# A list of 386 steps put in another order, with the PSUM pool and the copy engine of each step named anew (local attention beside a long convolution, one core)

## The chip, the core and the metric

The kernel runs on one core of a Trainium2 chip. The core has a matrix engine (PE, which multiplies and transposes, and writes to the memory PSUM alone), a vector engine (DVE), a scalar engine (ACT), a general engine (POOL) and a queue engine (SP) that here issues nearly all transfers (DMAs). Each engine works through its own instructions strictly in the order in which the program issues them, and waits for the others through semaphores. The metric is the device time of one execution in microseconds (us); lower is better.

## The reference, cut to what matters

The output has two halves of 576 columns for 2048 positions. The left half, A, is an attention with 32 heads of 18 columns in which each position looks at 8 positions, 2 apart, behind it. The right half, B, multiplies `q` with a causal convolution, as long as the sequence, of a short convolution of `k` times `v`.

```python
def _A_ref(x, wqkv, wo):                       # x: 1 x 2048 x 576
    H = 32; Dh = D // H; W, dil = 8, 2
    q, k, v = split(x @ wqkv)                  # 32 heads of 18
    idx = pos[:, None] - off[None, :]          # off = 0, 2, .. 14
    kg, vg = k[idx], v[idx]
    logits = einsum("bhsd,bhswd->bhsw", q, kg) * scale   # -1e9 where idx < 0
    o = einsum("bhsw,bhswd->bhsd", softmax(logits), vg)
    return o @ wo
def _B_ref(q, k, v, shift_k, ssm_k, ssm_D):    # each 1 x 2048 x 576
    k_shift = sum over 4 taps t of k_pad[:, t:t + S] * shift_k[:, 3 - t]
    kv = k_shift * v
    y = irfft(rfft(kv, 2S) * rfft(ssm_k, 2S))[:S]
    return q * (y + kv * ssm_D)
out = concatenate([A, B], axis=-1)
```

## The kernel before

The program is one straight line of instructions. It is not written out in loops but as a list, `ORDER` (lines 18 to 46), of 386 items; lines 718 to 724 go through it and call one small function per item, and every engine gets its instructions in that order (`manual_schedule`). An item such as `qk.1.0.3:bs` names the function (`qk`), its arguments (1, 0, 3) and after the colon up to two letters. `a` or `b` says from which of the two PSUM pools, `pa` or `pb` (lines 86 and 87, two buffers of two banks each), the step takes its tiles. `s` or `v` says which engine copies the result out of PSUM: `s` is ACT, `v` is DVE. Without a letter the step takes its default; for `evac` (line 101, most steps) that is ACT, for `copy32` (line 364, the transposes) and for `ys` it is DVE. A letter on a step that uses no PSUM, such as `cv.0.0:a`, has no effect.

The steps, by what they compute:

- `lx`, `lwq`, `lwv`, `lk`, `lv`, `lkn`, `lwo` load inputs through SP. `tj`, `tv`, `t0` to `t5`, `tw`, `ia`, `wt`, `sk` make tables; `ia` (line 434) has four PSUM tiles, transposed by PE, and six copies of them on ACT.
- A, first part: `xt.q.k` transposes x (line 369), `qk.comp.cp.j` projects queries (comp 0) or keys (comp 1) for half cp of the heads and quarter j of the positions (line 417), `qt` the remaining heads, `v.c.k` the values, which go to the DRAM buffer `Dv` and come back shifted through `vl` (line 410).
- A, logits: `lm.n.h` (line 513) is one product on DVE, q times shifted keys, into one of three slots `prr` (or, for h = 2, one of two slots `phr`); `lb.n` (line 526) sums it on PE, and frees the slots of `lm.n.0` and `lm.n.1` and after an odd n the `phr` slot. Then `at`, `sm.0.*` and `sm.1.*` (softmax for each half of the positions; `sm.*.4` is the Exp on ACT), `bt`.
- A, output: `pm.c.ct` (line 637) is a product on DVE of a loaded `vl` tile (three slots `vSr`, two `vStr`) with the weights, into one of three slots `Pr`; `ps` sums on PE and copies out; `po.c.t` multiplies by `wo`, copies to one of two slots `sAr`, and after each second one stores to the output.
- B, forward: `cv.c.k` (line 480) is the short convolution, 32 DVE instructions; `sx` and `kp` transform it and `ssm_k` on PE and write to the DRAM buffers `Dx` and `Dk` (`s1_part`, line 450); `kt` transposes `ssm_k` into two slots. `kl.i` and `xl.i` load a group back, each into one of four slots `Wr`; `ks.i.h` and `xs.i.h` (line 589, two PSUM tiles of 576 columns each) are the second transform.
- B, product and back: `gp.i.h` (line 612, two DVE instructions) multiplies the spectra, `gi.i.h` (line 621, two PSUM tiles) transforms back and stores to the DRAM buffer `Dy`; `yl.i` loads from it, again into a `Wr` slot; `ys.i.u` (line 695) is the last transform and the product with `q` on DVE, in one of two slots `ysr`, stored after u = 1. With the letter `s` ACT copies `ys` out first, and DVE multiplies from SBUF.

A slot is handed out when its step is reached in the list; its first writer then waits until the former user is done, for `ysr` and `sAr` until the former store has landed. SP issues transfers in list order and waits at each until its data or its slot is ready, with all later ones behind it.

Of the kernel before, what the change touches and what calls it, by code (L numbers as in the profile page):

```python
# [15 lines left out]


ORDER = """
lx.0 tj lx.1 lx.2 lwq.1 lwv wm.11 tv t0 xt.0.2:av sk:b lk.0 t2 xt.1.2:av lwq.0 xt.1.0:av xt.1.1:bv xt.0.0:s xt.0.1:bv
xt.2.1:s qk.1.1.1:bs xt.2.2:s t3 tw t1 lx.3 cv.0.0:a lv.1 lk.1 qk.1.1.0:bs cv.0.1:b cv.0.2:b cv.0.3:b qk.1.0.0:s  # L20
xt.2.0:as lv.0 v.0.1:b cv.0.4:b v.1.1:bs wt lk.3 v.0.0:a xt.3.0:s cv.0.5:b lk.2 cv.0.6:a cv.0.7:b cv.1.0 qk.0.1.0:b
xt.3.1:b t4 xt.3.2:as cv.1.1 lm.0.1 cv.1.2:b t5 cv.1.3:b qk.0.0.0:a sx.0.0:s qt.1:s cv.1.4:a lm.0.0 v.2.1:as lv.2
sx.1.0:a cv.1.5 cv.1.6 sx.0.1:b qt.0:b sx.0.2:a cv.1.7:a qk.0.1.1 sx.1.1 qk.0.1.3:b v.0.2:s v.1.2:bs lm.0.2 v.1.0:a
sx.1.2:b qk.1.0.1:bs sx.3.0:b cv.2.0:a qk.0.0.1:a v.3.1:a cv.2.1 sx.3.1 sx.2.0:s cv.2.2:a qt.3:as v.2.0:as qk.1.1.3:bs
sx.2.1:s cv.2.3:a lm.1.0 lb.0:a cv.2.4 cv.2.5:b v.2.2:bs cv.2.6 lm.1.1 v.3.2:av sx.2.2:b sx.3.2:b lv.3 cv.2.7:b
qk.0.1.2:a lb.1:b cv.3.0:b lm.2.2 cv.3.1 cv.3.2:b v.3.0:a qk.1.1.2:bs lm.2.1 qk.0.0.3:bs qk.1.0.3:bs lwo sx.4.0:a
cv.3.3:a lm.3.1 qt.2 sx.4.1:b sx.4.2 qk.0.0.2:as cv.3.4:b cv.3.5:b sx.5.0:b lm.2.0 qk.1.0.2 sx.5.1:a lb.2:bs cv.3.6
cv.3.7:a lm.6.0 at.0.0 lkn sx.5.2:av lm.4.2 ia:b lm.3.0 sx.6.0:as sx.6.1:as sx.6.2:s kt.3:b sx.7.0 sx.7.1:a sx.7.2:av
kt.1:bv lb.3:bs kp.1.0:bs kp.1.1:as lm.4.1 lm.4.0 kp.1.2:bs kp.3.0:s kt.0:as kp.3.1:b kp.3.2:s lm.6.2 kt.2:av lb.4:a
kp.0.0 kp.0.1:s lm.6.1 at.0.1 sm.0.0 xl.0 kp.0.2 kp.2.0:av lm.5.1 kp.2.1:s kp.2.2:bs kt.5:as kt.4:s sm.0.1 lb.6:a  # L30
kp.5.0:av kp.5.1:bs lm.5.0 sm.0.2 xl.1 kp.5.2:as kp.4.0:bs kt.6 kp.4.1:a kp.4.2:as sm.0.3 kt.7:s lb.5:s kp.6.0:as
xs.0.0:bv kp.6.1:a xl.2 kp.6.2:as kp.7.0:v kp.7.1:a kp.7.2 lm.7.0 sm.0.4 lm.7.1 xs.1.0:as sm.0.5 xs.0.1 xs.1.1:a
sm.0.6 lb.7:bs sm.0.7 kl.1 sm.0.8 kl.0 kl.3 ks.1.0:s sm.0.9 sm.0.11 sm.0.10 ks.1.1:as ks.0.0 gp.1.0 at.1.0:av vl.0.0
gp.1.1 bt.0.1:v ks.0.1:bs gp.0.0 ks.3.0:bs gi.1.0:as vl.0.1 xs.2.0:b xl.4 xs.2.1:as gp.0.1 xl.3 bt.0.0:bv at.1.1:b
vl.1.2 sm.1.0 ks.3.1:as kl.2 gi.1.1 pm.0.0 gi.0.0:s xs.3.0:a sm.1.1 vl.0.2 ks.2.0:b pm.0.1 xs.3.1:as sm.1.2 gp.3.0
vl.1.0 kl.4 sm.1.3 gi.0.1:bs gp.3.1 pm.0.2 xs.4.0:as gp.2.0 ks.2.1:b ps.0.0:a pm.0.3 sm.1.4 ks.4.0:b xl.7 gp.2.1 kl.7
gi.3.0:a ks.4.1:b gp.4.0 xs.4.1:as vl.1.1 gi.2.0:s pm.1.4 ks.7.0:a xl.5 pm.1.0 ps.0.1:bs ks.7.1:s vl.2.0 gp.4.1 pm.1.1
xs.5.0:as sm.1.5 sm.1.6 xs.7.0:b kl.6 kl.5 gi.2.1:a xs.7.1:bs ps.1.0:v xs.5.1:b ks.5.0:a vl.3.0 xl.6 gi.4.0 ps.1.2:a
gi.3.1:s vl.3.2 pm.1.2 gi.4.1:as ks.5.1:s pm.0.4 sm.1.7 gp.5.0 pm.1.3 sm.1.8 ps.0.2:bs gp.5.1 xs.6.0 yl.3 sm.1.9 yl.2
ps.1.1:a ks.6.0:s po.0.0:s xs.6.1:bs sm.1.10 gi.5.0:a gp.7.0 yl.0 vl.2.1 gi.5.1:bs gp.6.0 po.0.2:a sm.1.11 vl.2.2  # L40
gp.7.1 po.0.1 ys.3.0:v ys.3.1:v yl.1 bt.1.1:as bt.1.0 po.0.3:bs ks.6.1:bs pm.2.0 gi.7.0:as gi.7.1 gp.6.1 pm.2.1
gi.6.0:a po.1.0:bs pm.2.2 ps.2.0:a vl.3.1 gi.6.1:bs pm.2.4 ys.2.0:av ps.2.2:bs pm.2.3 ys.0.0:v ys.2.1:bs ys.0.1:as
po.1.2 ps.2.1:a po.1.1:b po.1.3:bs pm.3.4 pm.3.0 po.2.0 yl.6 yl.4 pm.3.1 po.2.1:s ps.3.0:b pm.3.2 ps.3.2:a po.2.2:b
pm.3.3 ys.6.0:as yl.5 ys.1.0:v ys.1.1:v ps.3.1:as ys.6.1:v po.2.3:v yl.7 po.3.0:a ys.5.0:bv ys.5.1:a po.3.1:b po.3.2:s
ys.4.0:v po.3.3:b ys.4.1:v ys.7.0:a ys.7.1:bs
"""


# [706 lines left out]
```

## Time and profile before

| | |
|---|---|
| median of the runs shown | 233.52 us (232.54 to 233.6, 3 runs) |
| the profiled execution, first to last instruction | 233.3 us |
| ACT busy | 164.7 us |
| PE granted clock, mean | 0.954 of full speed |
| moved by DMA | 60.57 MB, mean 260 GB/s |
| last `pm` ends on DVE | 213.57 us |

The profile page states for each engine the time in which it was busy, and other views tell what ended each wait. An engine that is busy nearly all the time, in the order of the list, sets the time of its stretch; an engine that waits does so for the last of what it needs. Busy time counts overlapping instructions once. The means of single instructions are a little longer than the distance between two of them, since an engine starts the next one before the last result is out.

### The profile page before, as it was taken

The page shows a single profiled execution, that of the slowest core. Times are in us where ns is not written, and L with a number is a line of the kernel's source. Part 1 is how long each engine was busy: PE and PEld are TensorE (multiplying, and loading weights), DVE is VectorE, ACT ScalarE, POOL GpSimd, SP SyncE. Part 2 cuts the span into 40 slices and gives each one's busy share as a digit, 9 for nine tenths or more (in the row PEclk, how much of TensorE's full clock was granted, in tenths as well). Part 3 has the DMA queues.
Part 4 walks back from the last instruction along what each step waited for, and adds up shares of the span by engine and source line. Part 5 has one row for each costly group of instructions (what it writes and reads, how often), then busy time and mean ns, then how long its engine had stood idle before and what let it go on. Part 6 is the DMA issues. An engine that isn't in the chain of part 4 may idle for free. (4 is left out here: it accounts for less than half of the span.)

```text
span 233.3 us, 4423 instructions
## 1 busy us (share of the span) xinstructions
PE 196.2 (84%) x1727; PEld 112.5 (48%) x1736; DVE 200.7 (86%) x199; ACT 164.7 (71%) x241; POOL 22.2 (10%) x53
## 2 busy tenths in 40 slices
PE   7899969999999977959873979668898979896981
PEld 2644524544544444545532456434564656564661
DVE  2679999989596999778969999999999999996533
ACT  2675739677754969487989789899999758535321
POOL 8001540110210110200000000000000010010100
PEclk9999999999999996779998599999999999997999
...
GB/s 221 348 276 393 248 85 106 155 162 48 55 198 268 134 273 327 218 221 211 307 290 207 330 353 326 374 355 400 306 360 299 327 332 379 274 275 339 121 272 214
DMA packets 46965, 60.57 MB, mean 260 GB/s; under 512 B 2368, under 2 KB 40064, under 8 KB 45920
## 3 DMA queue, kind: packets, MB, share of 16 engines
...
q14 instruction: 8, 0.07, 0.1%
...
## 5 line engine op out<-in xcount | busy, mean ns | idle before, releaser
L103 ACT ACTIVATE area<-psB 128x576 bf16<-128x576 f32 (+7 forms) x122 | 85.2, 745 | 32.2 <-PE psB L381 7.6
L103 ACT ACTIVATE area<-psA 128x576 bf16<-128x576 f32 (+7 forms) x105 | 75.6, 760 | 30.7 <-PE psA L381 12.0
L519 DVE TENSOR_TENSOR area<-area 128x4096 bf16<-128x4096 bf16 x16 | 36.4, 2285 | 5.7 <-PE psA L540 3.3
L642 DVE TENSOR_TENSOR area<-area,area 128x4096 bf16<-128x4096 bf16 (+1 forms) x20 | 40.7, 2069 | 0.1
L381 PEld LDWEIGHTS <-area 128*128 128x128 bf16 x160 | 15.5, 98 | 20.0 <-issue 3.0
L594 PEld LDWEIGHTS <-W 128*64 128x64 bf16 x256 | 14.1, 113 | 22.0 <-issue 15.0
L484 DVE TENSOR_TENSOR area<-area,area 128x2304 bf16<-128x2304 bf16 x16 | 21.6, 1362 | 0.8 <-PE psB L456 0.6
L594 PE MATMUL psB<-area,W 128*64 128x288 bf16 x160 | 16.2, 299 | 6.9 <-DMA area<-Dk 3.9
L381 PE MATMUL psB<-area,area 128*128 128x512 bf16 x85 | 20.1, 379 | 0.3
L693 POOL DMA_DIRECT2D area<-in_B_q_dram x8 | 6.0, 747 | 142.8 <-DVE area L706 119.2
L381 PE MATMUL psA<-area,area 128*128 128x512 bf16 x67 | 16.1, 379 | 2.7 <-DVE area L367 2.5
L456 PE MATMUL psB<-area,T 128*128 128x384 bf16 x58 | 14.8, 346 | 2.9 <-ACT area L103 2.7
L456 PEld LDWEIGHTS <-T 128*128 128x128 bf16 x96 | 9.3, 104 | 15.1 <-issue 9.2
L486 DVE TENSOR_TENSOR area<-area,area 128x2304 bf16<-128x2304 bf16 x12 | 16.3, 1356 | 0.3
L629 PEld LDWEIGHTS <-IAt 64*128 64x128 bf16 x256 | 12.4, 94 | 6.9 <-issue 4.0
L680 PEld LDWEIGHTS <-area 128*128 128x128 bf16 x128 | 12.4, 100 | 5.8 <-issue 2.6
L381 PE MATMUL psA<-area,wv 128*128 128x512 bf16 x60 | 13.9, 379 | 0.0
L594 PE MATMUL psA<-area,W 128*64 128x288 bf16 x96 | 10.2, 310 | 4.1 <-ACT area L103 3.6
L381 PEld LDWEIGHTS <-wv 128*128 128x128 bf16 x80 | 7.6, 98 | 9.4 <-issue 0.6
L616 DVE TENSOR_TENSOR area<-area 128x1152 bf16<-128x1152 bf16 x16 | 12.0, 749 | 0.0
L615 DVE TENSOR_TENSOR area<-area 128x1152 bf16<-128x1152 bf16 x16 | 11.9, 746 | 0.0
L456 PE MATMUL psA<-area,T 128*128 128x384 bf16 x38 | 10.0, 364 | 1.8 <-ACT area L103 1.7
...
## 6 DMA issues: line engine op xcount, KB each, us to landing
area<-Dv SPq DMA_DIRECT2D x8, 1054.0 KB, 8.0
...
area<-Dx SPq DMA_DIRECT2D x8, 576.0 KB, 5.7
area<-Dk SPq DMA_DIRECT2D x8, 576.0 KB, 5.3
Dy<-area SPq DMA_DIRECT2D x8, 576.0 KB, 4.6
area<-Dy SPq DMA_DIRECT2D x8, 576.0 KB, 7.0
...
```

Source lines behind the costliest of these rows:

```text
L103: nc.scalar.activation(dst, src, ACT.Copy, **({} if scale is None else {"scale": scale}))
L381: nc.tensor.matmul(ps[:, u, :], w[:, kb, cols[u]:cols[u] + 128], xT[:, kb, t], start=(kb == 0), stop=(kb == 4))
L456: nc.tensor.matmul(ps[:, ri, 0:384], T1[:, ri, :], sf[:, 384 * ch:384 * ch + 384], start=True, stop=not extra)
L484: nc.vector.tensor_tensor(tB if k else tA, kfull[:, 4 * c + 3 - j:4 * c + 7 - j, :], skb[:, j, :].unsqueeze(1).to_broadcast([128, 4, D]), ...
L486: nc.vector.tensor_tensor(tA, tA, tB, ALU.add)
L519: nc.vector.tensor_tensor(prr.get((n, h)), q2[h][:, :, 512 * aq:512 * aq + 512].unsqueeze(1).to_broadcast([128, 4, 2, 512]), kv, ALU.mult)
L594: nc.tensor.matmul(ps[64 * hp:64 * hp + 64, im, 0:HD], W2[:, im, 8 * g + 2 * prl + hp].rearrange("p l f -> p (l f)"), Wt[:, 2 * prl + hp, ...
L615: nc.vector.tensor_tensor(P[:, 0:2], X, K, ALU.mult)
L616: nc.vector.tensor_tensor(P[:, 2:4], X, swap, ALU.mult)
L629: nc.tensor.matmul(ps[:, hp, 0:HD], IAt[r, tab, 4 * g + 2 * hv + u, :], Pp[(i, hv)][r, n, u, :], start=(n == 0), stop=(n == 3), tile_posit ...
L642: nc.vector.tensor_tensor(P, vv, Lt[:, :, 512 * c:512 * c + 512].unsqueeze(2).to_broadcast([128, 2, nd, 512]), ALU.mult)
L680: nc.tensor.matmul(ps[:, di, 0:288], oT[:, 512 * ct + 128 * tt:512 * ct + 128 * tt + 128], wot[:, ct, d0:d1], start=(ct == 0), stop=False)
```

## The change

`ORDER` is replaced by another list of the same 386 steps. Nothing else in the program changes: no function, no tile, no pool and no transfer. Every step of the old list is in the new one; many stand elsewhere, and the letters after the colon differ for most steps that use PSUM. Of the copies out of PSUM these change engine: on DVE are 7 `xt` (6 before), 6 `kt` (4), 3 `ps` (1), 3 `po` (1), 1 `ks` (0), 1 `lb` (0), 1 `wt` (0), 2 `at` (4), and no `kp` (3), `sx` (2) or `v` (1) any more; `xs` (1) and `bt` (3) keep their number; 10 `ys` (4) are copied out by ACT first.

```diff
--- before.py
+++ after.py
@@ -16,33 +16,33 @@
 
 
 ORDER = """
-lx.0 tj lx.1 lx.2 lwq.1 lwv wm.11 tv t0 xt.0.2:av sk:b lk.0 t2 xt.1.2:av lwq.0 xt.1.0:av xt.1.1:bv xt.0.0:s xt.0.1:bv
-xt.2.1:s qk.1.1.1:bs xt.2.2:s t3 tw t1 lx.3 cv.0.0:a lv.1 lk.1 qk.1.1.0:bs cv.0.1:b cv.0.2:b cv.0.3:b qk.1.0.0:s
-xt.2.0:as lv.0 v.0.1:b cv.0.4:b v.1.1:bs wt lk.3 v.0.0:a xt.3.0:s cv.0.5:b lk.2 cv.0.6:a cv.0.7:b cv.1.0 qk.0.1.0:b
-xt.3.1:b t4 xt.3.2:as cv.1.1 lm.0.1 cv.1.2:b t5 cv.1.3:b qk.0.0.0:a sx.0.0:s qt.1:s cv.1.4:a lm.0.0 v.2.1:as lv.2
-sx.1.0:a cv.1.5 cv.1.6 sx.0.1:b qt.0:b sx.0.2:a cv.1.7:a qk.0.1.1 sx.1.1 qk.0.1.3:b v.0.2:s v.1.2:bs lm.0.2 v.1.0:a
-sx.1.2:b qk.1.0.1:bs sx.3.0:b cv.2.0:a qk.0.0.1:a v.3.1:a cv.2.1 sx.3.1 sx.2.0:s cv.2.2:a qt.3:as v.2.0:as qk.1.1.3:bs
-sx.2.1:s cv.2.3:a lm.1.0 lb.0:a cv.2.4 cv.2.5:b v.2.2:bs cv.2.6 lm.1.1 v.3.2:av sx.2.2:b sx.3.2:b lv.3 cv.2.7:b
-qk.0.1.2:a lb.1:b cv.3.0:b lm.2.2 cv.3.1 cv.3.2:b v.3.0:a qk.1.1.2:bs lm.2.1 qk.0.0.3:bs qk.1.0.3:bs lwo sx.4.0:a
-cv.3.3:a lm.3.1 qt.2 sx.4.1:b sx.4.2 qk.0.0.2:as cv.3.4:b cv.3.5:b sx.5.0:b lm.2.0 qk.1.0.2 sx.5.1:a lb.2:bs cv.3.6
-cv.3.7:a lm.6.0 at.0.0 lkn sx.5.2:av lm.4.2 ia:b lm.3.0 sx.6.0:as sx.6.1:as sx.6.2:s kt.3:b sx.7.0 sx.7.1:a sx.7.2:av
-kt.1:bv lb.3:bs kp.1.0:bs kp.1.1:as lm.4.1 lm.4.0 kp.1.2:bs kp.3.0:s kt.0:as kp.3.1:b kp.3.2:s lm.6.2 kt.2:av lb.4:a
-kp.0.0 kp.0.1:s lm.6.1 at.0.1 sm.0.0 xl.0 kp.0.2 kp.2.0:av lm.5.1 kp.2.1:s kp.2.2:bs kt.5:as kt.4:s sm.0.1 lb.6:a
-kp.5.0:av kp.5.1:bs lm.5.0 sm.0.2 xl.1 kp.5.2:as kp.4.0:bs kt.6 kp.4.1:a kp.4.2:as sm.0.3 kt.7:s lb.5:s kp.6.0:as
-xs.0.0:bv kp.6.1:a xl.2 kp.6.2:as kp.7.0:v kp.7.1:a kp.7.2 lm.7.0 sm.0.4 lm.7.1 xs.1.0:as sm.0.5 xs.0.1 xs.1.1:a
-sm.0.6 lb.7:bs sm.0.7 kl.1 sm.0.8 kl.0 kl.3 ks.1.0:s sm.0.9 sm.0.11 sm.0.10 ks.1.1:as ks.0.0 gp.1.0 at.1.0:av vl.0.0
-gp.1.1 bt.0.1:v ks.0.1:bs gp.0.0 ks.3.0:bs gi.1.0:as vl.0.1 xs.2.0:b xl.4 xs.2.1:as gp.0.1 xl.3 bt.0.0:bv at.1.1:b
-vl.1.2 sm.1.0 ks.3.1:as kl.2 gi.1.1 pm.0.0 gi.0.0:s xs.3.0:a sm.1.1 vl.0.2 ks.2.0:b pm.0.1 xs.3.1:as sm.1.2 gp.3.0
-vl.1.0 kl.4 sm.1.3 gi.0.1:bs gp.3.1 pm.0.2 xs.4.0:as gp.2.0 ks.2.1:b ps.0.0:a pm.0.3 sm.1.4 ks.4.0:b xl.7 gp.2.1 kl.7
-gi.3.0:a ks.4.1:b gp.4.0 xs.4.1:as vl.1.1 gi.2.0:s pm.1.4 ks.7.0:a xl.5 pm.1.0 ps.0.1:bs ks.7.1:s vl.2.0 gp.4.1 pm.1.1
-xs.5.0:as sm.1.5 sm.1.6 xs.7.0:b kl.6 kl.5 gi.2.1:a xs.7.1:bs ps.1.0:v xs.5.1:b ks.5.0:a vl.3.0 xl.6 gi.4.0 ps.1.2:a
-gi.3.1:s vl.3.2 pm.1.2 gi.4.1:as ks.5.1:s pm.0.4 sm.1.7 gp.5.0 pm.1.3 sm.1.8 ps.0.2:bs gp.5.1 xs.6.0 yl.3 sm.1.9 yl.2
-ps.1.1:a ks.6.0:s po.0.0:s xs.6.1:bs sm.1.10 gi.5.0:a gp.7.0 yl.0 vl.2.1 gi.5.1:bs gp.6.0 po.0.2:a sm.1.11 vl.2.2
-gp.7.1 po.0.1 ys.3.0:v ys.3.1:v yl.1 bt.1.1:as bt.1.0 po.0.3:bs ks.6.1:bs pm.2.0 gi.7.0:as gi.7.1 gp.6.1 pm.2.1
-gi.6.0:a po.1.0:bs pm.2.2 ps.2.0:a vl.3.1 gi.6.1:bs pm.2.4 ys.2.0:av ps.2.2:bs pm.2.3 ys.0.0:v ys.2.1:bs ys.0.1:as
-po.1.2 ps.2.1:a po.1.1:b po.1.3:bs pm.3.4 pm.3.0 po.2.0 yl.6 yl.4 pm.3.1 po.2.1:s ps.3.0:b pm.3.2 ps.3.2:a po.2.2:b
-pm.3.3 ys.6.0:as yl.5 ys.1.0:v ys.1.1:v ps.3.1:as ys.6.1:v po.2.3:v yl.7 po.3.0:a ys.5.0:bv ys.5.1:a po.3.1:b po.3.2:s
-ys.4.0:v po.3.3:b ys.4.1:v ys.7.0:a ys.7.1:bs
+lx.0 tj lx.3 lx.1 lwq.1 wm.11:a tv t2 t0 xt.0.1:bs xt.0.0:av xt.0.2:b sk:a lwq.0 xt.1.0:bs t5 lk.0 lwv xt.3.0:b
+xt.1.1:as lv.0 xt.3.1:as t3 qk.1.0.0:b t1 xt.3.2:b tw lx.2 cv.0.0 cv.0.1 qk.0.1.0:a lk.1 cv.0.2 wt:v xt.1.2:as cv.0.3
+t4 qk.0.0.0:b qk.1.1.1:b qk.1.1.3:a xt.2.0:bv cv.0.4 lk.2 cv.0.5 xt.2.2:bv cv.0.6 cv.1.0 qt.1:a xt.2.1:a qk.1.1.0:b
+cv.0.7 qt.0:a cv.1.1 qt.3:b cv.1.2 qk.0.0.1:a cv.1.3 sx.0.0:a lm.2.0 lv.2 qk.0.1.1:b v.0.0:b cv.1.4 cv.1.5 cv.1.6
+sx.0.1:b qk.1.0.3:a lm.0.0 lk.3 lm.0.2 lv.1 lm.0.1 sx.1.0:a qk.0.1.3:b sx.1.1:a sx.0.2:b cv.1.7 qk.1.0.1:a sx.1.2:b
+cv.2.0 cv.2.1 cv.2.2 qk.1.0.2:b v.0.1:a qk.1.1.2:a cv.2.3 v.0.2:b cv.2.4 v.1.2:a lb.0:b sx.2.0:a sx.2.1:b sx.2.2:a
+cv.2.5 v.1.0:b lm.1.1 sx.3.0:a qk.0.0.3:a cv.2.6 sx.3.1:b v.1.1:b sx.3.2:a v.2.0:b lm.1.0 cv.2.7 lv.3 cv.3.0 sx.4.0:a
+cv.3.1 lb.1:b lm.3.0 v.2.2:b v.3.2:a cv.3.2 sx.4.1:b sx.5.0:a lm.2.2 lm.2.1 v.2.1:b sx.4.2:a sx.5.1:b v.3.1:a v.3.0:b
+sx.5.2:bs cv.3.3 qt.2:a qk.0.1.2:a cv.3.4 qk.0.0.2:a cv.3.5 cv.3.6 lm.6.2 lb.2:b lwo cv.3.7 sx.6.0:a sx.7.0:a sx.6.1:b
+lkn lm.3.1 lb.3:b lm.4.2 sx.6.2:a lm.4.0 sx.7.1:b at.0.1:bs sx.7.2:bs at.0.0:as kt.6:as kt.3:bs kp.6.0:a xl.0 lm.4.1
+sm.0.0 lm.6.1 kp.6.1:b lb.4:a sm.0.1 kp.6.2:b lm.6.0 kp.3.0:a kp.3.1:a kt.1:b kp.3.2:a kt.7:a lm.7.0 lb.6:b sm.0.2
+kp.7.0:bs xl.6 kp.7.1:a lm.5.0 kp.7.2:b kt.5:bv kp.1.0:a kp.1.1:b kp.1.2:b sm.0.3 sm.0.4 xl.1 kp.5.0:bs kp.5.1:b
+lm.5.1 kt.2:a lb.5:av lm.7.1 sm.0.5 kp.5.2:a kp.2.0:as sm.0.6 kp.2.1:b kt.4:bv sm.0.7 kp.2.2:a kt.0:a lb.7:b xs.1.0:a
+sm.0.8 vl.1.0 kp.0.0:b kp.0.1:b kp.0.2:a at.1.0:a at.1.1:b kp.4.0:b kp.4.1:a kp.4.2:a sm.0.9 xs.0.0:bs vl.0.0 sm.0.10
+xs.1.1:a sm.0.11 sm.1.0 bt.0.0:b bt.0.1:b pm.1.0 pm.1.1 kl.0 xs.0.1:a pm.0.0 ia:b kl.1 ks.0.0:a ks.0.1:b ks.1.0:a
+sm.1.1 ks.1.1:b gp.0.0 ps.1.0:as xl.2 gp.0.1 gp.1.0 vl.0.1 vl.1.2 vl.0.2 xs.6.0:b gi.0.0:a gp.1.1 kl.6 sm.1.2 xl.4
+xs.6.1:b xs.2.0:a kl.2 pm.0.1 sm.1.3 vl.3.0 ks.6.0:b ps.0.0:a vl.1.1 gp.6.0 gi.0.1:b xs.2.1:av kl.3 ks.6.1:av sm.1.4
+ks.2.0:b xl.7 ks.2.1:b gi.1.0:a xl.3 gp.6.1 gi.1.1:b sm.1.5 gi.6.0:a pm.0.2 gp.2.0 gp.2.1 gi.6.1:b ks.3.0:a pm.1.4
+xs.3.0:b ks.3.1:a xs.4.0:b pm.0.3 vl.3.2 xl.5 sm.1.6 xs.4.1:a kl.4 ps.1.2:bv xs.3.1:b kl.7 gi.2.0:a vl.2.0 gp.3.0
+pm.0.4 vl.2.2 gi.2.1:b gi.3.0:a gp.3.1 ks.4.0:b gi.3.1:a ks.4.1:b ps.0.1:a ps.0.2:a ks.7.0:b pm.1.2 ks.7.1:a gp.4.0
+pm.1.3 gp.4.1 kl.5 ps.1.1:bv xs.7.0:a yl.3 sm.1.7 xs.5.0:b xs.7.1:a po.1.2:b ks.5.0:a sm.1.8 gp.7.0 sm.1.9 vl.2.1
+gi.4.0:b yl.0 gi.4.1:a gp.5.0 po.1.0:b sm.1.11 xs.5.1:a yl.2 sm.1.10 ks.5.1:b gp.7.1 bt.1.1:av yl.1 gp.5.1 ys.0.0:as
+bt.1.0:bs pm.2.0 po.1.1:b ys.0.1:a pm.2.1 po.1.3:b gi.7.0:a gi.7.1:b gi.5.0:a gi.5.1:b pm.2.4 vl.3.1 po.0.0:a po.0.1:a
+pm.2.2 ps.2.0:b yl.6 ps.2.2:a pm.2.3 pm.3.4 ys.2.0:as ys.2.1:b po.0.2:b pm.3.0 ps.2.1:a ys.3.0:as po.0.3:b yl.5
+po.2.0:b pm.3.1 ys.3.1:as yl.7 ys.1.0:bs po.2.2:b ps.3.0:b ps.3.2:a pm.3.2 ys.1.1:as po.2.1:b pm.3.3 ys.5.0:bs
+ys.5.1:as yl.4 po.2.3:as ps.3.1:av ys.7.0:as ys.7.1:bv ys.6.0:bv po.3.0:av po.3.1:av ys.6.1:bs po.3.2:bv ys.4.0:b
+po.3.3:a ys.4.1:a
 """
 
 
```

## Prediction, made before the changed kernel was run

> **What bounds the kernel now.** I read the page first, then the busy time by stretches, the waits of DVE, and the order of instructions in time. The new list gives the same work to the same engines, so what can change is waiting alone.
>
> ```profile
> span 233.3 us, 4423 instructions
> PE 196.2 (84%) x1727; PEld 112.5 (48%) x1736; DVE 200.7 (86%) x199; ACT 164.7 (71%) x241; POOL 22.2 (10%) x53
> ```
>
> DVE is the busiest engine, and its share is an average. By stretches (columns: length, busy PE, weight loads, DVE, ACT, POOL, granted clock, DMA share, GB/s):
>
> ```profile
> 26.00:133.10 107.10, 92.02 (x683) 48.05 (x690) 95.25 (x76) 78.29 (x106) 12.95 (x25) 0.92 0.67 201
> 133.10:213.60 80.50, 66.45 (x792) 42.32 (x789) 79.95 (x77) 65.69 (x111) 2.23 (x3) 0.99 0.96 336
> 213.60:233.30 19.70, 13.82 (x112) 9.80 (x110) 7.45 (x11) 5.57 (x8) 0.75 (x1) 0.93 0.72 214
> ```
>
> From 133.1 us to the last `pm` (213.6) DVE never stops: 79.95 of 80.5. Before that it idles 11.85 of 107.1 us, and behind it lies a tail of 19.7 us in which no engine is full. The waits of DVE (us in total, times, longest) and one of them in the order of time say why:
>
> ```profile
> DVE area L706 <- DMA out_dram<-area: 4.1, 1, 4.1
> DVE area L519 <- PE psA L540: 3.3, 2, 2.4
> DVE area L706 <- ACT area L103: 2.8, 1, 2.8
> DVE area L105 <- PE psA L456: 2.8, 2, 1.8
> DVE area L519 <- ACT area L103: 2.0, 2, 1.8
> ```
>
> ```profile
> 71.34 1.02 ACT L103 ACTIVATE area<-psB 128x1024 bf16<-128x1024 f32 x1 [1.09 <-PE psB L381]
> 72.40 2.29 DVE L519 TENSOR_TENSOR area<-area 128x4096 bf16<-128x4096 bf16 x1 [1.76 <-ACT area L103]
> ```
>
> `lm` waits for `lb` (L540) to free a slot. The second wait needs nothing: `lm.2.1` reads the first quarter of the keys, but starts when ACT's copy of `qk.1.1.2`, a later quarter of the same tile, is done (72.36). So an `lm` waits for every `qk.1` of its half listed before it.
>
> **The measure.** I add up, along each list, the row means of what DVE, ACT and PE do. Old list: DVE 211.2, ACT 186.0; new: DVE 210.6, ACT 188.2. A few copies on DVE have no row of their form: `lb` (512 columns) I take at 0.67 between 0.42 (256) and 0.75 (576); `wt` at 0.5 from the same two. DVE's listed work passes faster than its sum, since neighbours overlap: in the last stretch listed 85.6 take 79.95 busy, a factor of 0.934.
>
> **Stage 1, to listed 17.9 (`xt.2.0`): +1.3.** New, `xt.3.0` is copied by DVE before `t3`, and on PE it lies behind `sk`, whose third tile waits for ACT's first copy. `xt.0.1`'s copy (1.02) now lies before that on ACT, so `t3` starts near 11.6, not 11.50; its Sin waits for it; `tw` ends and `cv.0.0` starts at 18.7 (18.42 before), with 0.7 less DVE work done. `xt.2.0` costs another 0.4, as PE gets there at 25.2. Its loads do not decide: `lx.2` has 6.0 MB before and in it, some 20.5 us at the 302 GB/s of the first 24.6 us. DVE is at 25.9 where it was at 24.6. On POOL `lwv`'s memset (1.05) moves behind `t0`, so `ident` is ready earlier; it costs and gains nothing, since the first transposes wait for `lx.0` (5.94) and `ident` was there at 4.05. The loads of `q` on POOL wait for slots of `qtr`, four of them, as before.
>
> **Stage 2, to listed 117.9 (the first `pm`): -4.5.** Before: 108.5 us, 11.0 of them in waits of 0.2 us and more. I walk the new list with PE at 0.9 of its listed price (17.3 listed take 15.4 us from `lb.1` to `qk.1.0.2` before). No `lm` then finds a `qk.1` unfinished: the last two stand 4 and 8 us ahead. Waits I find: `lm.3.0` for `lb.1` 1.1; `lm.6.2` for `qt.2`, listed four steps ahead, 1.2; `lm.3.1` for `lb.2` 0.6; `lm.4.2` for `lb.3`, which needs the `lm.3.1` just before it, 0.7; `kt.7` for ACT's copy of `kp.3.1` 1.1; `at.1.0`, behind `xs.1.0` and `kp.0` on PE, 1.8. Together 6.5 for 11.0. Behind a waiting `lm` stand only `cv` and `sm`, whose readers (`sx`, `at`) have PE work ahead of them. Its bounds: no wait at all (-9.7 with stage 1) and as much as before (+1.3). `ia` (34 transposes on PE, six copies on ACT) leaves this stage. The first `pm` starts at 129.9, not 133.1.
>
> **Stage 3, to the last `pm`: +2.1.** `ia` moves here, after the third `pm`: six ACT copies at 0.91 (5 took 4.69), 5.5 us, covered by three `pm` (2.2 each, 6.7 in all). Uncovered it would delay `gp` by all of 5.5. Then ACT has 38 pairs of 576-column copies, and
>
> ```profile
> 157.19 1.34 ACT L103 ACTIVATE area<-psA 128x576 bf16<-128x576 f32 x2
> 158.25 1.36 ACT L103 ACTIVATE area<-psB 128x576 bf16<-128x576 f32 x2
> 159.31 1.39 ACT L103 ACTIVATE area<-psA 128x576 bf16<-128x576 f32 x2
> ```
>
> shows a pair each 1.06. With an Exp (1.8), three `ps` and small ones that is 47.7, against DVE's 52.8 x 0.934 = 49.3 up to `pm.2.0`: ACT nearly sets the pace, and in places does. `gp.0.0` waits for `ks.0.1` 0.9, `ps.1.2` on DVE 0.6, `gp.3.0` for `xs.3.1` 1.1, `gp.4.0` for `ks.4.1` 1.2. Behind `gp.0.0` stand `gp.0.1`, `gp.1` and `pm.0.1`; PE needs the first for `gi.0.0`, but has `xs.6.0` ahead of it. Listed 84.4 x 0.934 + 3.8 = 82.6, for 80.5. Bounds: ACT's pairs at 1.06 throughout and no wait, 78.8; each pair at the 1.19 of an unqueued one, 5 us more on ACT, 86.
>
> **Loads in stage 3: +1.9.** Between listed 118 and 140 the new list orders 9.6 MB, the old one 7.3; `vl.3.0`, used last of all, is fetched here. Before, 130 to 170 us ran at 357 GB/s (busy share 0.94), at which 9.6 MB take 26.9 us against 25.0 of DVE's way. Bounds: 0 (at 400 GB/s, the fullest slice of the page, 24 us) and 4 (at 330). I take the row with the same mixture. The Trainium skill ("DMA: Bandwidth & Descriptors", section "Where 436 GB/s comes from") names about 358 GB/s per core for the memory's side and 435 for the ports; by the first the term is 1.9, by the second 0, and this trace's slices up to 400 lie between.
>
> **The tail: -4.2.** Before, two stores lie on the chain that ended last:
>
> ```profile
> 205.75 5.31 DMA out_dram<-area
> ...
> 219.02 5.22 DMA out_dram<-area
> ```
>
> The second holds `ys.5.0`, which needs the slot of `ys.6`, stored just before. In the new list ten `ys` after the last `pm` become eight and halves of `ys`, `po` and `ps` go to ACT and DVE in turn. From the last `pm`: `ps.3.1` on PE 1.0, copied by DVE 1.2; `ys.6.0` waits for the store of `ys.5` (issued 1.2 us after the `pm`, 4.3 to landing), to +6.2; behind it on DVE the copies of `po.3.0` and `po.3.1` stand until +7.7; `ys.4.0` waits for the store of `ys.7` to +9.7; `ys.4.1` ends at +11.5; the last store lands 4.0 later. 15.5 for 19.7; with stores of 5.3 us, 18.2.
>
> **Sum.** -3.2 (stages 1 and 2) +2.1 +1.9 -4.2 = -3.4, and +0.9 for hand-offs below 0.2 us (stage 2 idled 11.85 with 11.0 in named waits): 230.8 for 233.3. The profiled execution lies 0.2 under the median, so 231.0.
>
> **Rivals.**
> *Loads late (slower).* SP issues in list order, and a `Wr` slot is only refilled when its reader on PE is done. `xl.6` takes one of four slots some 20 us before the others, and `vl.3.0` one of three `vSr` slots until the end. That leaves `xl.3` 6.8 us and `kl.4` 6.1 us from slot to use; `kl.3` and `kl.5` are alike.
>
> ```profile
> area<-Dv SPq DMA_DIRECT2D x8, 1054.0 KB, 8.0
> ...
> area<-Dx SPq DMA_DIRECT2D x8, 576.0 KB, 5.7
> area<-Dk SPq DMA_DIRECT2D x8, 576.0 KB, 5.3
> ```
>
> The loads of 576 KB from `Dx` and `Dk` take 5.7 and 5.3 us; if the crowd lifts them above 6, each comes late, at 8.0 (the big `Dv` loads) by some 1.8; behind a late `ks` stand PE's later steps, ACT's copies of them and then `gp` and `pm`, so four of them add up to 7 us: 238. For it: the bytes. Against: DMA already ran at 0.96 with DVE at 99%. Chance 0.30.
> *The tail stays.* Stores of 5.3 us keep it at 18.2: 233.7. For it: the two on the chain; against: the median of 3.7. Chance 0.17.
> *No crowd.* Without the load term and the hand-offs: 228.2. Chance 0.13.
> That the change does nothing can't be: the list is the order of issue. The letters on `cv` fall away without effect.
>
> **How the numbers follow.** My forecast has 0.40; its own range is 229 to 233.5. About 0.5% (1.17 us) is what a measurement tells from no change, so faster is below 232.35, slower above 234.7. Faster: 0.32 of the forecast, 0.13 without crowd, 0.04 of the tail, 0.49. Same: 0.08 + 0.06 = 0.14. Slower: 0.30 + 0.07 = 0.37. The range, 227 to 239, leaves out the ends of the first rival and of the third.
>
> **What would show it.** Right: first `pm` on DVE near 130; an `lm` never released by ACT's copy of a `qk.1`; `ia` beside three `pm`; DVE idle about 4 us from there to the last `pm` near 214; a tail near 15.5, its waits on stores. Wrong: waits of PE (L594) on `Dk` or `Dx` above 3 us in stage 3 (first rival), or PE behind DVE by more than the named waits in stage 2, which my walk would not see.

## The result, and the profile after

The changed kernel takes 244.75 us (median of 4 runs, 243.15 to 247.37); the kernel before, beside it on the same chip, 233.03 (4 runs, 232.28 to 233.6). The ratio is 1.05, interval 1.0427 to 1.0573: slower by 11.7 us, where a gain of 2.5 had been forecast. Below, medians leave out two executions above 310 us (the profiled one of the single letter and one of `lb.4` ahead) and hold one of 375.63 us of the kernel before, while ratios and their intervals leave out every execution more than 1.5% above the fastest of its kernel, so that the two can differ by a microsecond. The page of the changed kernel begins:

```profile
span 243.7 us, 4442 instructions
...
PE 200.8 (82%) x1736; PEld 115.2 (47%) x1736; DVE 199.6 (82%) x202; ACT 166.2 (68%) x244; POOL 21.7 (9%) x53
```

DVE and ACT are as busy as before to within 1.5 us; PE is busy 4.6 us longer with the same work. The busy time by stretches, cut at the prediction's marks (copy of `xt.2.0`, first `pm`, end of the last `pm`; columns as in the prediction), of the changed kernel:

```profile
24.50:140.30 115.80, 96.70 (x691) 48.99 (x691) 96.05 (x75) 75.80 (x103) 11.82 (x17) 0.91 0.64 186
140.30:229.20 88.90, 72.73 (x822) 48.23 (x820) 79.01 (x78) 72.83 (x121) 2.24 (x3) 0.92 0.92 322
229.20:243.70 14.50, 9.85 (x88) 7.01 (x86) 8.00 (x13) 3.10 (x5) 0.75 (x1) 1.00 0.75 225
```

| | before | predicted | after |
|---|---|---|---|
| to listed 17.9 (`xt.2.0`) | 24.6 | 25.9 | 24.5 |
| from there to listed 117.9 (the first `pm`) | 108.5 | 104.0 | 115.8 |
| from there to the last `pm`, loads included | 80.5 | 84.5 | 88.9 |
| tail | 19.7 | 15.5 | 14.5 |

The marks are amounts of listed work on DVE. In the kernel before, 133.1 us is where DVE has done as much listed work as stands ahead of the new list's first `pm`; its own first `pm` comes later, at 143.37. The column before is of an execution of 235.0 us (every time on record lies 1.7 us above its span), so the columns add up to 10.4 us between them and not to the 11.7 of the medians.

So most was lost ahead of the first `pm`, where the forecast had its gain. The longest waits of DVE and PE in the changed kernel (us in total, times, longest):

```profile
DVE area L519 <- PE psA L540: 8.2, 1, 8.2
...
PE psA L501 <- DMA area<-in_B_ssm_k_dram: 6.5, 4, 2.7
...
DVE area L519 <- ACT area L103: 5.4, 1, 5.4
...
PE psB L381 <- DVE area L367: 4.4, 2, 4.0
```

In the first, `lm.6.0` waits for `lb.4`; in the third `lm.0.0` waits for a `qk.1`, which no `lm` was to do. Behind each stands a wait of PE, and the experiments below show that these two cost most of what was lost.

*PE's wait for a copy.* In the order of time, DVE and PE of the changed kernel:

```profile
25.38 0.61 PE L375 MATMUL psA<-ident,area 128*128 128x128 bf16 x8
...
25.83 0.81 PE L381 MATMUL psB<-area,area 128*128 128x512 bf16 x3
...
28.64 1.35 DVE L484 TENSOR_TENSOR area<-area,area 128x2304 bf16<-128x2304 bf16 x1
...
29.91 0.68 DVE L367 TENSOR_SCALAR area<-psA 128x512 int32<-128x512 int32 x1
...
30.65 3.15 PE L381 MATMUL psB<-area,area 128*128 128x512 bf16 x7 [4.01 <-DVE area L367]
...
47.59 2.29 DVE L519 TENSOR_TENSOR area<-area 128x4096 bf16<-128x4096 bf16 x1 [5.43 <-ACT area L103]
```

The copy at 29.91 is that of `xt.2.1`. PE had transposed it by 26, but on DVE it stands behind the instructions of several `cv`, and `qk.1.1.0` on PE waits for it from 26.6 to 30.65. It does not need it: `qk.1.1.0` reads the first quarter of the positions, and `xt.2.1` writes the third, which PE reads from 51.96 on (`qk.1.0.2`). The wait is of the kind that the prediction found for `lm.2.1`. `xT` holds five blocks of 2048 columns, and `xt.2.1` writes columns 1024 to 1535 of blocks 2 and 3; of the matmuls of `qk.1.1.0` those on blocks 0, 1 and 2 run, and the fourth, the one on block 3, waits (x3 and x7 above). In the same way the second matmul of `qt.1` waits for `xt.2.0`. That fits a dependency taken over the whole stretch from the first column written to the last, which includes the first quarter of block 3; no run takes the dependency away. The seven matmuls that follow take 3.15 us, 0.45 each; ten of the same form take 2.32 at 37.06. The stretches of that time, of the changed kernel, say why (the granted clock is the third figure from the right):

```profile
26.60:30.60 4.00, 0.04 (x1) 0.00 (x0) 4.00 (x6) 0.36 (x2) 0.00 (x0) 0.85 0.00 0
30.60:36.10 5.50, 5.45 (x13) 1.92 (x13) 5.43 (x5) 1.16 (x2) 0.00 (x0) 0.50 0.37 109
36.10:42.00 5.90, 5.90 (x29) 2.77 (x28) 5.83 (x4) 4.23 (x8) 0.00 (x0) 0.99 0.00 0
```

After the hole of 4 us the clock is 0.50 for 5.5 us, in which PE does work of 2.75: the hole costs 4.0 + 2.75, and 0.87 more for a wait on `xt.2.0`'s copy before it, 7.6 in all. PE is then full to 88 us and makes up nothing.

*The late load.* SP, PE and DVE of the changed kernel:

```profile
91.44 4.50 SPq L264 DMA_DIRECT2D area<-in_B_ssm_k_dram  x5
...
104.29 0.33 PE L501 MATMUL psA<-ident,area 128*128 128x128 bf16 x1 [2.72 <-DMA area<-in_B_ssm_k_dram]
...
110.42 2.29 DVE L519 TENSOR_TENSOR area<-area 128x4096 bf16<-128x4096 bf16 x1 [8.24 <-PE psA L540]
```

`ssm_k` is ordered at 91.44 (82.39 before): its place is free only when PE, now late, has done the last projection, and `lwo` stands ahead of it on SP. `kt.6` (L501) follows at once on PE, where `ia` stood in between before, and waits 6.5 us for it in four pieces; `lb.4` stands behind `kt.6` and `kt.3`, and `lm.6.0` behind `lb.4`. The first load from `Dk`, which needs all of it, is then issued at 141.82 (127.42 before), and the first `gp` starts at 148.3 (134.9).

### The profile page after: what moved, and what is told of

It reads as the page before. It is cut to its first block, busy times and chain, and to the rows that moved or that the text cites. A ratio compares the mean times of both kernels' runs of the same rounds, so it can differ in the third digit from the quotient of the medians.

```text
span 243.7 us, 4442 instructions
## 1 busy us (share of the span) xinstructions
PE 200.8 (82%) x1736; PEld 115.2 (47%) x1736; DVE 199.6 (82%) x202; ACT 166.2 (68%) x244; POOL 21.7 (9%) x53
## 4 chain that ended last, share of the span: by engine, by line
PE 39%; DMA 31%; ACT 12%; DVE 8%; issue 7%; SPq 1%; DVEq 0%; ACTq 0%
ACT area L103 10%; PE psB L381 9%; DMA Dx<-area 7%; DMA area<-Dk 7%; PE psA L381 6%; DMA out_dram<-area 5%; DMA area<-in_B_v_dram 4%; DMA area<-in_A_wqkv_dram 3%; DMA area<-Dx 3%; PE psA L456 3%; PE psB L456 3%; PE psB L594 2%; DMA Dk<-area 2%; PE psA L594 2%; PE psA L629 2%
## 5 line engine op out<-in xcount | busy, mean ns | idle before, releaser
L103 ACT ACTIVATE area<-psA 128x576 bf16<-128x576 f32 (+9 forms) x120 | 83.9, 740 | 32.4 <-PE psA L381 7.9
L103 ACT ACTIVATE area<-psB 128x576 bf16<-128x576 f32 (+5 forms) x111 | 80.4, 765 | 36.6 <-PE psB L381 14.9
L381 PE MATMUL psB<-area,area 128*128 128x512 bf16 x70 | 17.9, 404 | 4.4 <-DVE area L367 4.4
L381 PE MATMUL psA<-area,area 128*128 128x512 bf16 x90 | 20.7, 379 | 0.0
L594 PE MATMUL psA<-area,W 128*64 128x288 bf16 x128 | 13.5, 319 | 3.7 <-DMA area<-Dk 1.2
L456 PE MATMUL psB<-area,T 128*128 128x384 bf16 x46 | 12.2, 351 | 4.3 <-ACT area L103 4.2
L680 PE MATMUL psB<-wv,area 128*128 128x288 bf16 x80 | 13.4, 297 | 1.3 <-ACT area L103 1.3
L615 DVE TENSOR_TENSOR area<-area 128x1152 bf16<-128x1152 bf16 x16 | 12.0, 749 | 3.1 <-ACT area L103 3.0
L381 PE MATMUL psB<-area,wv 128*128 128x512 bf16 x60 | 13.9, 379 | 0.0
L456 PE MATMUL psA<-area,T 128*128 128x384 bf16 x50 | 12.1, 333 | 0.9 <-ACT area L103 0.5
```

What stands on the lines that cost most here:

```text
L103: nc.scalar.activation(dst, src, ACT.Copy, **({} if scale is None else {"scale": scale}))
L381: nc.tensor.matmul(ps[:, u, :], w[:, kb, cols[u]:cols[u] + 128], xT[:, kb, t], start=(kb == 0), stop=(kb == 4))
L456: nc.tensor.matmul(ps[:, ri, 0:384], T1[:, ri, :], sf[:, 384 * ch:384 * ch + 384], start=True, stop=not extra)
L594: nc.tensor.matmul(ps[64 * hp:64 * hp + 64, im, 0:HD], W2[:, im, 8 * g + 2 * prl + hp].rearrange("p l f -> p (l f)"), Wt[:, 2 * prl + hp, ...
L615: nc.vector.tensor_tensor(P[:, 0:2], X, K, ALU.mult)
L680: nc.tensor.matmul(ps[:, di, 0:288], oT[:, 512 * ct + 128 * tt:512 * ct + 128 * tt + 128], wot[:, ct, d0:d1], start=(ct == 0), stop=False)
```

## The experiments

The kernels are timed beside the kernel before; its medians were 233.91 us (first set), 233.00 (second), 233.09 (third) and 232.45 (fourth).

**The copies of xt.2 on ACT.**

```diff
-xt.2.0:bv ... xt.2.2:bv ... xt.2.1:a
+xt.2.0:bs ... xt.2.2:bs ... xt.2.1:as
```

> The new list, with the copies of xt.2.0, xt.2.1 and xt.2.2 on ACT and not on DVE (3 letters). Theory A (in the new kernel PE waits 4.0 and 0.9 us at 24 to 31 us for these copies, which stand on DVE between the cv, and everything that PE does up to the load of ssm_k comes that much later): the two waits go, lm.0.0 waits under 1.5 us and not 5.4, the load of ssm_k is issued near 87 and not 91.4, the time falls by 3 to 5 us, to about 240. Rival B (the end is set by the loads in the stretch of the products, whatever comes before): the waits go too, but the time falls by less than 1 us.

236.69 us (235.94 to 239.57), ratio 1.0112 (1.0053 to 1.0171). Three letters take back 8.1 of 11.7 us by the medians and 9.0 by the ratios, more than I had given them, since I had not yet seen the clock behind the hole. Both waits of PE and that of `lm.0.0` are gone, `ssm_k` is ordered at 85.00; `lm.6.0` still waits 7.3 for `lb.4`.

**One of the three.**

```diff
-xt.2.1:a
+xt.2.1:as
```

> The changed kernel with one letter other: xt.2.1 is copied by ACT, not by DVE behind six cv; xt.2.0 and xt.2.2 stay on DVE. Theory A (this one copy ended 4 us after PE needed it, and PE, full from there to 88 us, never made it up): most of what the three letters brought, -6 to -7 of 8.1; PE's wait of 4.0 gone, the load of ssm_k issued near 86. Rival D (the three copies cost DVE's own time, 0.68 each and the waits beside them): a third of it, -2.7.

236.43 (median of three, 235.79 to 238.29), ratio 1.0197 (1.0137 to 1.0256). By the ratios, 1.05 and 1.0197, that is 7.1 us less (9.0 with three letters), by the medians 8.3 (8.1). One copy of 0.68 us, in its place in DVE's queue, makes most of the first cause. That its wait is gone is not shown by a trace of this kernel; only the time speaks. Rival D, DVE's own time, falls: a third was expected of it.

**DVE's wait alone.**

```diff
-sx.0.1:b qk.1.0.3:a lm.0.0 lk.3 lm.0.2 lv.1 lm.0.1 sx.1.0:a
+sx.0.1:b lm.0.0 lk.3 lm.0.2 lv.1 lm.0.1 qk.1.0.3:a sx.1.0:a
```

> The new list, with qk.1.0.3 moved from ahead of lm.0.0 to behind lm.0.1. Theory A with the needless dependency (lm.0.0 waits for the copy of a later quarter of the keys): lm.0.0 no longer waits 5.4 us; but PE does the same work in the same time, so the load of ssm_k comes where it was and the time falls by under 1.5 us: DVE's wait moves to the next lm that waits for lb. If DVE's own work set the time (theory of the prediction), it would fall by about 5 us.

243.71 (243.1 to 244.49), ratio 1.0414 (1.0357 to 1.0471): -1.0 by the medians, -2.0 by the ratios. The wait of 5.4 us of `lm.0.0` disappears and the time moves little: `cv.1.7` now waits 3.5 for a load of `v`, which SP issues right behind a store that needs PE's values (44.40 us), and `lm.6.0` waits 6.8. DVE's longest waits show where PE is late; they are not what is to be mended.

**The load of wo behind that of ssm_k.**

```diff
-cv.3.6 lm.6.2 lb.2:b lwo cv.3.7
+cv.3.6 lm.6.2 lb.2:b cv.3.7
...
-kt.5:bv kp.1.0:a
+kt.5:bv lwo kp.1.0:a
```

> The new list, with lwo (six transfers on SP) moved from directly ahead of the load of ssm_k to behind kt.5. Theory A: ssm_k is issued some 3 us earlier (88.5, set by the last projection on PE), kt.6 waits 3 to 4 us less for it, lm.6.0 waits about 5 us and not 8.2, the time falls by 2 to 4 us. Rival B: less than 1 us. If SP is not what holds the load (its slots are), the issue moves by less than 1 us and so does the time.

241.35 (240.29 to 243.34), ratio 1.0331 (1.0263 to 1.04): -3.4, as theory A has it. `ssm_k` is ordered at 87.27, PE waits 1.9 for it, `lm.6.0` 2.9, and the first `pm` starts at 135.8.

**The tables of ia as cover.** `ia` moves from behind the first three `pm` to the place where PE waits for `ssm_k`.

```diff
-at.0.0:as kt.6:as
+at.0.0:as ia:b kt.6:as
```

> The new list, with ia moved back to where the old list has it in kind: behind at.0.0, ahead of the first kt, while ssm_k is on its way. Theory A (kt waits 6.5 us for ssm_k because nothing stands between): PE does ia in this wait, lb.4 and lm.6.0 come no later than before (wait 7 to 9 us), and the first gp no longer has ia's 5.6 us of ACT ahead of it; it gains only if ia and not the load of the first Dk group (landed at 146.3) held gp: 0 to 1 us. Rival C (ia in the product stretch costs its ACT time): it falls by 4 to 6 us.

241.81 (241.09 to 243.52), ratio 1.0352 (1.0291 to 1.0413): -2.9, between the two theories. PE's wait for `ssm_k` is filled, but DVE waits 8.9 for `ia`'s last tile (a fifth one, besides the four copied on ACT, which DVE copies itself) and PE 6.1 on the first load from `Dk`.

**Both causes taken out.** The first and the fourth edit together.

> Both edits at once: the three copies of xt.2 on ACT, and the load of wo behind kt.5. Theory A (PE was held by DVE's copies of xt.2, and the load of ssm_k arrives late behind that of wo with nothing for PE between it and kt.6): alone the edits brought 8.1 and 3.4 us, but the first already moves the issue of the ssm_k load from 91.4 to 85.0, so they overlap: 233 to 235 us, the wait of lm.6.0 on L540 down from 7.3 to about 3, first pm near 130. Rival C (what is left after the copies is the amount of PE and ACT work around kp, not the landing of ssm_k): no further gain, 236 to 237, with PE's wait on ssm_k gone but ACT or PE busy throughout.

234.01 (231.29 to 236.04, 10 runs), ratio 1.004 (0.998 to 1.01). Four edits of 386 steps take back 10.7 of 11.7 us, and the result can't be told from the kernel before. The edits alone brought 8.1 and 3.4 by the medians, 9.0 and 3.9 by the ratios, so they overlap by 0.8 to 2.2. Of this kernel, the stretches at the same marks, and two at the time of the former hole:

```profile
24.50:128.80 104.30, 92.50 (x683) 47.99 (x688) 94.87 (x73) 77.61 (x106) 11.40 (x17) 0.93 0.70 208
128.80:215.10 86.30, 71.77 (x836) 48.89 (x834) 78.92 (x79) 73.80 (x122) 2.24 (x3) 0.94 0.95 330
215.10:232.60 17.50, 10.40 (x72) 6.90 (x71) 7.89 (x12) 1.95 (x3) 0.75 (x1) 0.87 0.63 182
```

```profile
26.60:30.60 4.00, 3.95 (x19) 1.76 (x18) 3.96 (x4) 3.92 (x8) 0.00 (x0) 1.00 0.00 0
30.60:36.10 5.50, 5.50 (x27) 2.54 (x26) 5.43 (x5) 3.40 (x5) 0.00 (x0) 1.00 0.39 109
```

PE is full and its clock 1.00. The second stage takes 104.3 us, where the prediction's walk had 104.0; DVE idles 9.4 of it. `qk.0.0.1`, the first `qk` behind the former hole, starts on PE at 29.30 instead of 37.06: 7.8 us, for the 7.6 counted above. `lm.6.0` still waits 3.5, as expected, and `ssm_k` is ordered at 79.46.

**lb.4 ahead of the transposes.** The kernel of the last run, with PE's order changed so that no sum of logits stands behind `kt.6`.

```diff
-at.0.0:as kt.6:as kt.3:bs kp.6.0:a xl.0 lm.4.1 sm.0.0 lm.6.1 kp.6.1:b lb.4:a sm.0.1
+at.0.0:as xl.0 lm.4.1 sm.0.0 lm.6.1 lb.4:a kt.6:as kt.3:bs kp.6.0:a kp.6.1:b sm.0.1
```

> As the run before, and lb.4 stands ahead of kt.6, kt.3, kp.6.0 and kp.6.1 on PE, so that no sum of logits stands behind a transpose that waits for ssm_k. Theory A: the wait of lm.6.0 on L540 is below 1 us and the first pm on DVE comes about 3 us earlier, but the chain over ssm_k, Dk and the first kl is as long as before, so the time moves by -1 to -3 against the run before. Rival C (the chain over ssm_k sets the first gp, DVE's wait is only a symptom): within 0.5 us of the run before, the wait reappears in front of the first gp.

233.3 (median of nine, 231.62 to 236.2), ratio 1.0048 (1.0005 to 1.0091): against the run before -0.7 by the medians and +0.2 by the ratios, no difference. The wait of `lm.6.0` is gone, but the first `pm` starts at 128.6 instead of 128.8, since three copies of `kt` on DVE now wait 1.6, 1.4 and 1.7 ahead of it. That is rival C's time, though it had the wait return in front of the first `gp`: with `ssm_k` early, DVE's wait was a symptom.

**A big load later.** On the kernel with both causes taken out:

```diff
-sm.1.3 vl.3.0 ks.6.0:b
+sm.1.3 ks.6.0:b
...
-vl.2.1 gi.4.0:b
+vl.2.1 vl.3.0 gi.4.0:b
```

> As the first run of this set, and the load vl.3.0 (1054 KB) moves from the third pm to behind vl.2.1, some 35 us later. Rival B (the prediction's rival of late loads: bytes ahead of xl.3, kl.3 and kl.4 make these late): the waits of L594 on Dx and Dk shrink from about 7 us to 4, time -2 to -3 against the first run. Theory A': the loads are late because their Wr slots are freed late, not because of the bytes: -0.5 to +0.5.

233.73 (231.15 to 235.04), ratio 1.0024 (0.9979 to 1.0069): -0.3, no difference. PE's wait on `Dx` shrinks from 2.2 to 1.6 and DVE's wait behind it from 2.3 to 0.7, but then PE waits 6.0 on a load from `Dy`, and DVE 3.8 behind that. Rival B, the bytes of `vl.3.0`, falls.

**Three loads better placed.** The kernel with `lb.4` ahead, with `vl.3.0` later as above, and:

```diff
-ks.2.0:b xl.7 ks.2.1:b gi.1.0:a xl.3
+ks.2.0:b xl.3 ks.2.1:b gi.1.0:a xl.7
...
-ys.1.1:as po.2.1:b pm.3.3 ys.5.0:bs ys.5.1:as yl.4
+ys.1.1:as yl.4 po.2.1:b pm.3.3 ys.5.0:bs ys.5.1:as
```

> The list of e6_lb4_first with three loads moved: vl.3.0 behind vl.2.1, xl.3 and xl.7 change places (xl.3 is used first), yl.4 directly behind ys.1.1. Theory H (what the repaired list still loses from the first gp on are three late loads: PE's 2.1 us wait on Dx, some of the 2.3 on Dy, and the 3.2 us of DVE in the tail): 230.5 to 232, faster than the kernel before by 0.5 to 1%. Rival I (these waits lie beside ACT's pace of copies, or turn into others, as moving vl.3.0 alone did): 233 to 234.

235.41 (232.27 to 238.09, 12 runs), ratio 1.008 (1.0034 to 1.0125): by the ratios 0.7 us above the kernel without these moves (1.0048), and the intervals overlap; by the medians 2.1, timed on another chip. Theory H falls, and rival I's 233 to 234 is missed too, on the slow side. The trace shows no wait of PE on `Dx` above 1 us any more, and one of 5.0 on `Dy` instead; but its execution, at 232.45, is one of the fastest of the twelve, so it does not show where the others lose time. That stays open.

**The new end in the kernel before.** The last 30 steps, from `pm.3.4` on, in the changed order with its letters, but for the loads `yl.6` and `yl.5`, which stand behind `po.2.0`; the beginning of it:

```diff
-pm.3.4 pm.3.0 po.2.0 yl.6 yl.4 pm.3.1 po.2.1:s ps.3.0:b pm.3.2 ps.3.2:a po.2.2:b pm.3.3 ys.6.0:as
+pm.3.4 pm.3.0 po.2.0:b yl.6 yl.5 pm.3.1 yl.7 ys.1.0:bs po.2.2:b ps.3.0:b ps.3.2:a pm.3.2 ys.1.1:as
...
```

> The kernel before with the last 30 steps (from pm.3.4 on) in the changed kernel's order with its letters. The prediction's tail term (ten ys after the last pm become eight, halves go to ACT and DVE in turn): the tail is 15 to 16 us for 19.7 and the time 228.5 to 230.5. Rival (the tail is short in the changed kernel only because its stage 3 was long and the back transforms were done by then): 232 to 234.

236.01 (233.97 to 236.54), ratio 1.0123 (1.0041 to 1.0205): slower by 3.0. Its last `pm` ends at 221.2, and the span at 234.8: the tail is 13.6 for 19.7, shorter than I had claimed. But the `ys` that have left it stand between the last `pm`s, and DVE waits there for ACT's copies of them:

```profile
213.27 0.46 DVE L706 TENSOR_TENSOR area<-area,area 128x576 bf16<-128x576 bf16 x1 [3.08 <-ACT area L103]
213.64 2.28 DVE L642 TENSOR_TENSOR area<-area,area 128x4096 bf16<-128x4096 bf16 x1
218.63 0.46 DVE L706 TENSOR_TENSOR area<-area,area 128x576 bf16<-128x576 bf16 x1 [2.71 <-ACT area L103]
```

So 6.1 us saved behind the last `pm` are 7.6 lost ahead of it (213.57 to 221.2). Neither account is right as it stands. The tail is short here too, so it is not short only because the changed kernel's stage 3 was long; but what the order saves behind the mark it loses ahead of it, and the time is above even the rival's 232 to 234.

**The second cause put into the kernel before**, its two steps together and apart.

```diff
-qk.0.0.3:bs qk.1.0.3:bs lwo sx.4.0:a
+qk.0.0.3:bs qk.1.0.3:bs sx.4.0:a
...
-at.0.0 lkn sx.5.2:av lm.4.2 ia:b lm.3.0
+at.0.0 lwo lkn sx.5.2:av lm.4.2 lm.3.0
...
-bt.0.1:v ks.0.1:bs
+bt.0.1:v ia:b ks.0.1:bs
```

> The kernel before with two steps of the changed list: lwo directly ahead of lkn in SP's queue, and ia taken from between lkn and kt.3 to behind bt.0.1. Theory A (the second cause): the load of ssm_k lands some 4 us later, PE waits for it and what stands behind (lb.4 and lm.6.1 or lm.5) with it; +2 to +4, 235 to 237. Rival E (ia itself costs more where it now stands, beside the first gp, than it covered): PE's wait on ssm_k stays under 1 and the loss lies behind the first pm.

244.61 (243.11 to 245.67), ratio 1.0547 (1.0495 to 1.0599): +11.5, far above the 2 to 4 expected and as much as the whole change. Both theories are seen at once: PE waits 5.0 on `ssm_k`, the first `gp` starts at 139.6 instead of 134.9, and there ACT has `ia` to do. Apart, first `lwo` alone, then `ia` alone:

> The kernel before with lwo alone moved directly ahead of lkn. Theory A (late ssm_k): with ia still between lkn and kt.3 most of it is covered, +1 to +3 of the 11.5 us that the two steps cost together. Rival J (the 1.5 MB of wo at this place delay the Dx stores behind them and all that follows): +5 or more.

236.9 (234.69 to 237.57), ratio 1.0185 (1.0105 to 1.0265): +4.4. The loads of `wo` are 720 KB, not the 1.5 MB named there. That is above theory A's 3 and below rival J's 5. PE waits 3.1 on `ssm_k` though `ia` is there, and the first `gp` starts at 136.5, 1.6 later; the profiled execution is the fastest of four, and its span, 233.0, is no longer than that of the kernel before (233.3), so the rest of the 4.4 was not found in it.

> The kernel before with ia alone moved behind bt.0.1. Theory A: lwo is early, so ssm_k lands as before and PE has only its own gap to wait, +1 to +2 there; beside the first gp ia takes 5.6 us of ACT that no pm covers: +4 to +5 in all. Rival E2 (the two steps add nothing to each other): this run and the run before add up to 11.5.

239.59 (238.02 to 241.38), ratio 1.0343 (1.0257 to 1.0429): +7.1, and with 4.4 that makes 11.6 of 11.5: the two add (rival E2). `ssm_k` makes PE wait 1.4 and the first `gp` starts at 135.1, as before. ACT's view of this kernel:

```profile
135.03 5.61 ACT L103 ACTIVATE IAt<-psB 128x1024 bf16<-128x1024 bf16 x6 [0.15 <-PE psB L440]
...
148.57 1.19 ACT L103 ACTIVATE area<-psB 128x576 bf16<-128x576 f32 x2
```

The six copies of `ia` stand in a row at the moment when the product starts. The pair that ran at 143.44 in the kernel before, behind the same row of four copies, runs at 148.57: 5.1 us later, with no `pm` on DVE to lie beside it. That is the prediction's price for an uncovered `ia`, 5.5.

**The better beginning with the old end.** The list of the kernel with `lb.4` ahead up to the first `pm`, then the remaining steps in the order of the kernel before, with three `pm` (not the two named below) and `ia` drawn ahead; three loads of the first part are exchanged for those that the old end needs first:

```diff
+pm.0.0 xs.0.1:a kl.1 pm.0.1 ia:b kl.0 vl.0.2 kl.3
 ks.1.0:s ks.1.1:as ks.0.0
+pm.0.2
 gp.1.0 gp.1.1 ks.0.1:bs gp.0.0 ks.3.0:bs gi.1.0:as
...
```

> The list of e6_lb4_first up to the first pm, then the remaining steps in the order and with the letters of the kernel before (two pm and ia moved ahead to cover the loads from Dk). Theory F (the changed list is better by 4 us up to the first pm, and worse by 3 to 4 from there to the end, so that the repaired list only equals the kernel before): first pm near 128.6, from there 100 to 101 us as before, 229 to 230.5 us, faster than both. Rival G (what the head gains, the tail takes back whatever its order, since Dk is stored later against the first pm than before): 232 to 234.

234.27 (232.89 to 237.91, 12 runs), ratio 1.0081 (1.0041 to 1.0121): rival G, a little above its 232 to 234. The first `pm` starts at 128.2, the first `gp` at 136.3, and from 142.4 to 150.3 DVE waits 8.0 for ACT. The `pm` that were drawn ahead filled a gap and are missing later, when ACT is full with copies of `ks`, `xs` and `gi` and DVE has nothing to lie beside them. No order that I tried is faster than the kernel before.

## Why the prediction was wrong

**Stage 1** was forecast at 25.9 and ended at 24.5, as before; the wait for Sin was smaller (`cv.0.0` at 18.2, not 18.7).

**Stage 2 is the step that failed**: -4.5 forecast, +7.3 measured. Two sentences of it were wrong. The first is "I walk the new list with PE at 0.9 of its listed price ... No `lm` then finds a `qk.1` unfinished: the last two stand 4 and 8 us ahead." The walk gave PE one rate throughout and no wait for the copies of `xt.2`; that `xt.2.0`, `xt.2.1` and `xt.2.2` are now copied by DVE, between `cv` that keep DVE full, stood in the list of letters and was not put into the walk. PE lost 7.6 us to it, so the margins of 4 and 8 us were gone. One letter brings 7 to 8 us back, three 8 to 9. The prediction had seen with `lm` that a step can wait for a later quarter of the tile that it reads; it did not ask the same of `qk` and the copies of `xt`.

The second is "`ia` (34 transposes on PE, six copies on ACT) leaves this stage", told without a price for what it covered. It had been the work that PE did while `ssm_k` was on its way. `lwo`, moved directly ahead of `lkn` on SP, was not mentioned at all, though SP issues in list order. Together with PE's delay they let `ssm_k` land with nothing to cover it: 3.4 us for `lwo`, 2.9 for `ia` when moved alone. With the copies and `lwo` mended, the sum of the walk comes out, 104.3 us for 104.0, but in part by luck: DVE idles 9.4 us where waits of 6.5 were named, and the three copies are no longer its work.

**Stage 3 and the tail** were forecast at 84.5 and 15.5, together 100.0. The changed kernel took 103.4 and the mended one 103.8 (86.3 and 17.5), so 3.4 to 3.8 us are missing whatever happens ahead. In stage 3 DVE idles 9.9 us in the changed kernel and 7.4 in the mended one, where 3.8 of waits and 1.9 for loads had been forecast; in the mended one the copy of `ps.1.2` alone waits 2.3, for 0.6 named, behind PE's wait on `Dx`. That `ia` is covered by three `pm` holds: in the mended kernel no wait of DVE stands at it, and uncovered it costs 5.1 on ACT. Loads and stores lie on the chain that ended last in the changed kernel, among them:

```profile
141.82 4.49 DMA area<-Dk
...
164.13 6.82 DMA area<-Dx
...
215.08 7.32 DMA out_dram<-area
```

But no run bears out the term for the bytes of the loads: moving the 1054 KB of `vl.3.0` away changed nothing (-0.3), and ordering a `Dx` load sooner, with two others, brought nothing. One late load gave way to another. The other 1.3 MB of the 2.3 that the new list orders more there were moved by no run, and what makes up the missing 3.4 to 3.8 us stays open.

**The tail** was forecast 4.2 shorter and measured 5.2 shorter, and was still no gain. I booked it by a mark, the last `pm`, past which the new list moves two `ys` and their waits. In the kernel before the same end saves 6.1 behind the mark and loses 7.6 ahead of it. In the mended kernel the tail is 17.5, near the 18.2 of the rival "The tail stays", and a copy on DVE waits 3.5 in it for a store.

**From span to time** the prediction took the profiled execution as 0.2 under the median. It compared a span with a time; that execution took 235.0 us, 1.5 above the median. The forecast gain of 2.5 us is a difference and does not depend on it.

**The rivals.** "Loads late" had the right side, and its 238 lies nearer than the forecast, but its sign did not show (the longest wait of PE on `Dk` or `Dx` in the changed kernel is 2.1 us, not above 3), and its place holds at most the 3.4 us after the first `pm`; of the 12.9 us by which the sum was short (230.8 for 243.7), 10.4 lie ahead of it (129.9 for 140.3), and 0.9 of hand-offs goes the other way. The last sentence of the prediction named the true case, PE behind DVE in stage 2 by more than the named waits, "which my walk would not see", and gave it no chance and no price.
